# Loads of x in 2 KB instead of 8 KB descriptors, on a newly planned order of a fused attention and feed-forward kernel

## The chip, the cores and the metric

One core of one Trainium2 chip. The metric is the time of one execution in microseconds (us) on the device, lower is better. Before: 150.68 us as the median of 3 runs (150.09 to 151.19). The runs of this kernel scatter with the clock that TensorE is granted; a run is called fast when it is within 1.5% of the fastest of the same kernel, and ratios are taken over fast runs alone.

## The reference

```python
def _attn_ref(x, inducing):                 # x (4, 12480, 128), inducing (32, 128)
    def mab(q, kv):
        s = scale * (q @ kv.transpose(0, 2, 1))
        a = softmax(s)                      # cut: written out with max, exp, sum
        return a @ kv
    h = mab(I, x)                           # I: inducing for each of the 4 batches
    return mab(x, h)

def _moe_ref(x, w_in, w_out, alpha):        # 49920 tokens, d_ff 2048
    h = x @ w_in
    g = np.maximum(h, 0.0) + alpha * np.minimum(h, 0.0)
    return g @ w_out
```

The kernel reads x once (25.56 MB of float32), pools each batch into 32 rows, and then makes the output of each batch (25.56 MB in all) from the scores of x against those rows. A batch's outputs cannot begin before all of its x has been pooled.

## The kernel before

A batch is cut into seven chunks: six of 2048 rows (1 MB of x) and one of 192. For each chunk the first phase is: load with a cast to bf16 (POOL issues it), transpose ("flip") on DVE, scores on TensorE, exponential on ACT, sums on TensorE. The second phase makes scores again, exponentials, and the output, which DVE, or ACT with POOL, moves from PSUM into a buffer `ob` that SP stores.

The order of instructions is not written by hand. A small planner in the kernel plays the program through with its own costs, before anything is built, and writes each engine's instructions in the order that came out. On the chip each engine works in that order, whatever the real durations are.

```python
RINGS = dict(xn=12, xt=10, p=7, h=1, e1=3, e1t=3, g=3, ob=5)     # buffers
CAPS = dict(A=2, S=2, F=7, O=5)
class Plan:
    HOP = 0.12                              # us from one engine to another
    RATE = dict(L=424e3, S=400e3)           # bytes per us of loads, of stores
    SHARE = dict(L=0.8, S=0.2)              # when both run
    # ... cut: play() picks, again and again, the ready task of highest priority
TA, TS, TB, WL, LEAD = 4.0, 0.6, 4.2, 10, 0 # pace of the phases, sets priorities

def load(_):
    v["xn"] = ring("xn")                    # xn: [P, NK=16, C=128] bf16
    nc.gpsimd.dma_start(
        out=v["xn"][: c.p, : c.nk, :],
        in_=x[s.b, c.t0 : c.t0 + c.n, :].rearrange("(p j) c -> p j c", p=c.p),
    )

def flip(_):
    xT = ring("xt")
    nc.vector.transpose(out=xT[...], in_=v["xn"][: c.p, : c.nk, :].bitcast(f32))
```

A partition's 16 rows are contiguous in HBM and in SBUF, so a load is 128 descriptors of 8 KB read (4 KB written). A store's runs are 2 KB.

The softmax here doesn't subtract the row's maximum and nothing guards it: scores larger than these inputs give would overflow.

## Time and profile before

| | before |
|---|---|
| median of the first 3 runs | 150.68 us |
| profiled run (slow), span | 154.58, 152.3 us |
| x loads: issue on POOL, to landing (median) | 0.56 us, 11.3 us |
| DVE's idle time that x ended | 4.4 us |
| first and last output stored (issue) | 43.0, 143.8 us |

In the groups of instructions a row has the line, engine and operation, what it writes and reads, the count, the busy time in us and the mean of one in ns, and behind the last bar the idle time of the engine just before such an instruction, with what ended most of it. These rows are the flips and the issues of loads:

```profile
L472 DVE STREAM_TRANSPOSE xt<-xn 128x1024 f32<-128x1024 f32 (+1 forms) x28 | 29.8, 1075 | 4.4 <-DMA xn<-in_x_dram 4.4
L465 POOL DMA_DIRECT2D xn<-in_x_dram x28 | 15.6, 560 | 10.5 <-DMA xn<-in_x_dram 9.7
```

The prediction shows the rest: DMA full until the loads end, first with loads alone, then with loads and stores.

### The profile page before, as it was taken

The numbers are of one execution on the slowest core, as the hardware profiler recorded it, in microseconds if no ns is written. First come the engines' busy times: TensorE is split into PE (matmuls) and PEld (weight loads), VectorE is DVE, ScalarE is ACT, GpSimd is POOL, SyncE is SP. The second block draws the span as 40 slices with busy tenths as digits, with TensorE's granted clock in tenths as the row PEclk, the third lists the DMA queues.
The fourth block names the chain that finished last, engine by engine and source line by source line (L and its number), as shares of the span: only waits on it lengthen the run. The fifth ranks groups of instructions, "written<-read, shape, count | busy, mean of one in ns | idle before, by whom it ended". The sixth has DMA issues, their size and how long they took to land. (4 is left out here: it accounts for less than half of the span.)

```text
span 152.3 us, 5852 instructions
## 1 busy us (share of the span) xinstructions
PE 110.2 (72%) x2474; PEld 60.5 (40%) x2474; DVE 94.9 (62%) x251; ACT 77.6 (51%) x190; POOL 93.4 (61%) x119
## 2 busy tenths in 40 slices
PE   0019987999985876899969699798979994565100
PEld 0012434555543433545445364355653553443000
DVE  2069783489867964569876579928785846373300
ACT  3001422554875765353876647645964966646200
POOL 7821212920577979723697679614994897999700
PEclk9999999999999999689999999999996999655555
DMA  3999999999999999999999999998199888689991
GB/s 37 200 216 211 215 210 214 215 216 213 209 226 214 343 273 336 404 284 247 220 251 242 371 268 271 363 281 315 66 377 374 306 298 289 238 305 386 376 363 37
DMA packets 18063, 39.89 MB, mean 262 GB/s; under 512 B 1136, under 2 KB 2416, under 8 KB 18032
## 3 DMA queue, kind: packets, MB, share of 16 engines
q0 software_dynamic: 4192, 13.83, 47.0%
q1 hardware_dynamic: 13648, 25.57, 46.4%
q8 instruction: 21, 0.34, 0.8%
q10 hardware_dynamic: 192, 0.07, 0.2%
q14 instruction: 10, 0.08, 0.1%
HBM read 27.73 MB, written 25.56 MB: 350 GB/s over the span
## 5 line engine op out<-in xcount | busy, mean ns | idle before, releaser
L884 POOL TENSOR_TENSOR ob<-ob,rd 128x512 f32<-128x512 f32 (+1 forms) x78 | 72.2, 954 | 33.9 <-ACT ob L871 33.8
L871 ACT COPY ob<-p 128x512 f32<-128x512 f32 (+1 forms) x78 | 37.7, 549 | 15.2 <-PE p L854 9.6
L317 PE MATMUL p<-xt,ind_t 32*32 32x512 bf16 (+1 forms) x432 | 27.3, 366 | 12.6 <-DVE xt L472 11.6
L472 DVE STREAM_TRANSPOSE xt<-xn 128x1024 f32<-128x1024 f32 (+1 forms) x28 | 29.8, 1075 | 4.4 <-DMA xn<-in_x_dram 4.4
L317 PE MATMUL p<-xt,bh 32*32 32x512 bf16 (+1 forms) x432 | 29.0, 381 | 3.2 <-issue 2.9
L484 ACT ACTIVATE e<-p 128x512 bf16<-128x512 f32 (+1 forms) x28 | 15.1, 551 | 22.4 <-PE p L317 20.3
L465 POOL DMA_DIRECT2D xn<-in_x_dram x28 | 15.6, 560 | 10.5 <-DMA xn<-in_x_dram 9.7
L644 ACT ACTIVATE e<-p 128x512 bf16<-128x512 f32 (+1 forms) x28 | 15.2, 546 | 12.2 <-PE p L317 12.0
L869 DVE TENSOR_TENSOR ob<-p,rd 128x512 f32<-128x512 f32 (+1 forms) x30 | 19.1, 652 | 0.5 <-PE p L854 0.5
L849 PE MATMUL p<-zb,e 32*128 32x128 bf16 (+1 forms) x396 | 12.7, 231 | 8.9 <-ACT g L841 5.1
L317 PEld LDWEIGHTS <-ind_t 32*32 32x32 bf16 x432 | 9.3, 92 | 22.8 <-DVE ind_t L336 9.5
L834 DVE RECIPROCAL rd<-p 128x16 f32<-128x16 f32 (+1 forms) x28 | 6.7, 239 | 18.6 <-PE p L828 14.1
L317 PEld LDWEIGHTS <-bh 32*32 32x32 bf16 x432 | 10.4, 93 | 11.1 <-issue 4.2
L849 PEld LDWEIGHTS <-e 32*128 32x128 bf16 (+1 forms) x396 | 7.5, 98 | 14.8 <-issue 14.2
L492 DVE STREAM_TRANSPOSE e1t<-e 128x256 f32<-128x256 f32 (+1 forms) x28 | 10.5, 379 | 3.7 <-ACT e L484 3.7
L653 DVE SCALAR_TENSOR_TENSOR h<-e,h 128x256 int32<-128x256 int32 (+1 forms) x28 | 10.6, 379 | 2.9 <-PE h L512 1.4
L854 PE MATMUL p<-wb,g 32*128 32x512 bf16 (+1 forms) x108 | 11.6, 397 | 0.0
L502 PE MATMUL h<-xn,e1t 128*32 128x128 bf16 x392 | 10.4, 225 | 1.5 <-DVE h L653 0.9
L823 PE MATMUL p<-e,sp 128*128 128x128 bf16 (+1 forms) x100 | 10.9, 231 | 0.0
L841 ACT ACTIVATE g<-p 128x128 bf16<-128x128 f32 (+1 forms) x28 | 8.0, 287 | 4.3 <-DVE rd L834 4.3
L823 PEld LDWEIGHTS <-sp 128*128 128x128 bf16 (+1 forms) x100 | 6.3, 102 | 9.3 <-issue 8.9
L502 PEld LDWEIGHTS <-e1t 128*32 128x32 bf16 x392 | 6.4, 97 | 7.1 <-issue 2.5
(104 smaller groups left out, 108.2 us busy)
## 6 DMA issues: line engine op xcount, KB each, us to landing
out_dram<-ob SPq DMA_DIRECT2D x24, 1024.0 KB, 7.7
xn<-in_x_dram POOLq DMA_DIRECT2D x24, 512.0 KB, 11.3
w_in_b<-in_moe_w_in_dram POOLq DMA_DIRECT2D x1, 512.0 KB, 16.4
WO<-in_moe_w_out_dram POOLq DMA_DIRECT2D x1, 512.0 KB, 17.3
out_dram<-ob SPq DMA_DIRECT2D x4, 96.0 KB, 5.7
xn<-in_x_dram POOLq DMA_DIRECT2D x4, 48.0 KB, 11.2
ind<-in_inducing_dram ACTq DMA_DIRECT2D x4, 16.0 KB, 3.4
al<-in_moe_alpha_dram SPq DMA_DIRECT2D x1, 8.0 KB, 2.1
```

The lines of the kernel that those rows point to most:

```text
L317: nc.tensor.matmul(sc[rows, :], rows_t[rows, bb, :, e], xT[rows, : c.nk, bb, :, e], start=(n == 0), stop=(n == 3),)
L465: nc.gpsimd.dma_start(out=v["xn"][: c.p, : c.nk, :], in_=x[s.b, c.t0 : c.t0 + c.n, :].rearrange("(p j) c -> p j c", p=c.p),)
L472: nc.vector.transpose(out=xT[: c.p, : c.nk].rearrange("p k b j e -> p (k b j e)").bitcast(f32), in_=v["xn"][: c.p, : c.nk, :].bitcast(f32),)
L484: nc.scalar.activation(out=v["e1"][: c.p, : c.w].rearrange("p (K j e) -> p K j e", j=M, e=2), in_=v["sc"][: c.p, :].rearrange("p (K e j) - ...
L502: nc.tensor.matmul(h_all[q * M : (q + 1) * M, :], v["e1t"][: c.p, k // 2, :, k % 2], v["xn"][: c.p, k, :], start=(c.i == 0 and k < G), sto ...
L644: nc.scalar.activation(out=s.e2[: c.p, c.off : c.off + c.w].rearrange("p (r j k) -> p r j k", j=M, k=c.nkk), in_=w["sc"][: c.p, :].rearran ...
L823: nc.tensor.matmul(hh[:, : c.po], SP[r][: c.p, q].rearrange("p a q f -> p (a q f)"), e2(q), start=(q == 0), stop=(q == c.nq - 1),)
L849: nc.tensor.matmul(v["o"][a][: c.po, q * C : (q + 1) * C], e2(q, rows[a]), ZB[r][rows[a], :], start=(q == 0), stop=False,)
L854: nc.tensor.matmul(v["o"][a][: c.po, : c.nq * C], v["g"][rows[a], : c.po], WB[r][rows[a], : c.nq].rearrange("p q c -> p (q c)"), start=Fal ...
L869: nc.vector.tensor_tensor(out=ob, in0=o, in1=spread(rd), op=ALU.mult)
L871: nc.scalar.copy(out=ob, in_=o)
L884: nc.gpsimd.tensor_tensor(out=ob, in0=ob, in1=spread(s.rd[: c.po, c.i, : c.nq, a]), op=ALU.mult,)
```

## The change

The title names the descriptors, but two things change at once.

1. The tile of a load is padded, four runs of 512 elements and 2 spare ones each. A partition's 8 KB then cannot be one run in SBUF, and becomes four descriptors of 2 KB read and 1 KB written. The intent is that loads and stores, taken in turn packet by packet, share the DMA engines equally.
2. The order is planned anew: TensorE's results cost 0.2 us to another engine and a change of its tile mode 0.1, its groups are given other durations, filler matmuls stay in the running mode, rings and caps differ, and ten constants are set anew.

```diff
-RINGS = dict(xn=12, xt=10, p=7, h=1, e1=3, e1t=3, g=3, ob=5)
-CAPS = dict(A=2, S=2, F=7, O=5)
+RINGS = dict(xn=10, xt=14, p=7, h=1, e1=3, e1t=3, g=3, ob=5)
+CAPS = dict(A=2, S=3, F=7, O=5)
-LATE = 90.0
-AP = -0.2
-BIAS = 0.4
+LATE = 55.0
+AP = 0.0
+BIAS = 0.8
-    HOP = 0.12
+    HOP = 0.07
+    DRAIN = 0.2
+    SWITCH = 0.1
...
+                if eng == "PE":
+                    end += self.SWITCH if t["mode"] != self.mode else 0.0
+                    self.mode = t["mode"]
...
-        xn=([P, NK, C], bf16), ...
+        xn=([P, 4, NK // 4 * C + 2], bf16), ...
-    FB = 10.0
+    FB = 3.0
-    TA, TS, TB, WL, LEAD = 4.0, 0.6, 4.2, 10, 0
+    TA, TS, TB, WL, LEAD = 4.0, 1.2, 5.0, 6, 1
...
+        def rows_of(xn, c):
+            return xn[: c.p, : c.nkk, : c.nq * C]
-                out=v["xn"][: c.p, : c.nk, :],
-                in_=x[s.b, c.t0 : c.t0 + c.n, :].rearrange("(p j) c -> p j c", p=c.p),
+                out=rows_of(v["xn"], c),
+                in_=x[s.b, c.t0 : c.t0 + c.n, :].rearrange("(p k r) c -> p k (r c)", p=c.p, k=c.nkk),
...
-        XP = 10.0
+        XP = 40.0
... (cut: the planner's durations of the TensorE groups, each with its mode now)
```

SHARE stays at 0.8 and 0.2: the planner still believes that a load beside a store gets four fifths.

## The prediction

> **What bounds the kernel now.** I began with the page's row of DMA use by slice and the row of GB/s under it. A load counts there with the bf16 bytes that it writes, half of what it reads from HBM.
>
> ```profile
> PE   0019987999985876899969699798979994565100
> POOL 7821212920577979723697679614994897999700
> PEclk9999999999999999689999999999996999655555
> DMA  3999999999999999999999999998199888689991
> GB/s 37 200 216 211 215 210 214 215 216 213 209 226 214 343 273 336 404 284 247 220 251 242 371 268 271 363 281 315 66 377 374 306 298 289 238 305 386 376 363 37
> ```
>
> A slice is 3.8 us. From slice 2 to slice 28 the 16 DMA engines are full, to about 105 us. Until 43 us only loads run, at some 212 GB/s written, 424 read. Then loads and stores share. After the last load (landed at 103.5 us) only stores are left and the DMA row has holes: there the making of outputs is the bound. I then cut the span at those points with the view of busy time by stretch (PE, PEld, DVE, ACT, POOL, clock, DMA share, GB/s):
>
> ```profile
> 24.00:43.00 19.00, 17.45 (x368) 9.23 (x369) 14.51 (x35) 10.13 (x24) 8.84 (x9) 1.00 1.07 214
> 43.00:75.00 32.00, 26.32 (x653) 14.87 (x656) 21.92 (x57) 18.67 (x49) 21.54 (x27) 0.95 1.03 288
> 75.00:104.00 29.00, 24.82 (x618) 13.79 (x614) 20.77 (x53) 18.18 (x44) 20.70 (x25) 1.00 1.04 294
> 104.00:112.00 8.00, 6.53 (x188) 3.95 (x186) 6.26 (x21) 6.24 (x17) 6.06 (x7) 1.00 0.54 197
> 112.00:130.00 18.00, 15.59 (x315) 8.71 (x311) 11.98 (x38) 12.06 (x32) 14.30 (x17) 0.91 0.87 314
> 130.00:144.00 14.00, 6.80 (x114) 4.51 (x112) 6.07 (x14) 7.26 (x19) 12.91 (x14) 0.52 0.91 337
> ```
>
> Before 104 us the DMA share is 1.03 to 1.07. Behind it no engine sits at its limit: each waits for another in a fixed order. In the last 14 us POOL is busy 12.91 of 14. This profile fell in a slow state (154.58 us, against 150.68 as the median of the timed runs), and the granted clock of 0.52 at its end is part of that; I take some 4 us off the tail in a fast run.
>
> The third view is the DMA view of single stretches: loads alone (8 to 18 us), both (89 to 93), stores alone (112 to 119). Columns: packets, MB, share of 16 engines.
>
> ```profile
> q0 software_dynamic: 582, 2.12, 105.7%
> ```
> ```profile
> q0 software_dynamic: 170, 0.63, 77.9%
> q1 hardware_dynamic: 171, 0.35, 25.6%
> ```
> ```profile
> q1 hardware_dynamic: 1322, 2.61, 102.1%
> ```
>
> Queue 0 is the loads, queue 1 the stores. When both have work they take turns packet by packet, 170 to 171, and since a load packet reads 8 KB and a store packet carries 2 KB, loads get four fifths of the traffic (78% of the time against 26%).
>
> **What the Trainium skill says.** "DMA: Bandwidth & Descriptors", section "Queues, rings and completion order", says that each DMA engine goes round its queues at packet granularity; 170 against 171 agrees. The same page, "Why small descriptors are slow", gives a fixed overhead of about 3 cycles a packet, and the page's table a fabric of 32 bytes a cycle at 850 MHz on each engine. By that a 2 KB packet takes 67 cycles, 78.8 ns, and an 8 KB one 259 cycles, 304.7 ns: the trace has 309 (10 us x 16 / 517 full packets) for 8 KB, close, but 88 for the stores' 2 KB (7 us x 16 / 1274), more than the page's. "TensorEngine Tiling (Array Packing)", "Key Properties", says that changing the tiling mode drains TensorE. This trace does not isolate it; the planner in the new kernel now charges 0.1 us for it.
>
> **The change, part by part.**
>
> *Descriptors.* 24 full x loads have 128 packets of 8 KB, 8 per DMA engine and load, 192 in all: 192 x 309 ns = 59.3 us. They become 768 of 2 KB. At the page's 79 ns that is 60.5 us, at the stores' 88 ns 67.6. The stores write HBM and loads read it, so I choose 82, an estimate: 63.0 us, **+3.7 us of DMA time**. 14 full loads land before 46 us, where only loads run and DVE and TensorE follow them closely: 14 x 8 x 19 ns = 2.1 us on the path. The other 1.6 us fall where DMA is full too, so they move the last load as well.
>
> *Shares.* With equal packets loads and stores get half each. The total of bytes is the same, so where DMA is full this only changes the order: stores land sooner, loads later. At 103.5 us some 1.5 MB of stores were still under way; with equal shares perhaps half of that, so the last load is later by 0.75 MB / 380 = **+2 us**. Nobody waits in the trace for an output buffer, so faster stores free nothing.
>
> *Issue.* POOL takes 530 to 540 ns for a load of 128 descriptors and 522 to 530 for one of 96. From that slope 512 would cost about 0.12 us more (an estimate), 3 us over all loads, beside other work.
>
> *The new plan.* The order view shows the same sequence with small moves: 16 loads before the first output in both, the last load issued about one output earlier, one more output group after the last sums of the pooling. One output's transfer fewer ahead of the last load is 1.05 MB / 375 = **-2.8 us** there, and up to one chunk more in the tail, where a chunk takes 40 us / 14 = 2.9: zero in sum. Evictions by POOL fall from 78 to 70, by DVE they rise from 30 to 37, one is done by ACT in four scaled pieces. In the last two batches POOL loses 2 of 31 large ones, 2 x 1.05 = **-2 us** where it is the busiest engine.
>
> *Truer costs of TensorE in the planner* (drain 0.2 instead of 0.12 us to another engine, 0.1 for a mode switch, shorter sums). These cannot speed an instruction, only put fewer waiting instructions at the head of a queue. Waits of that kind between 43 and 104 us, from the view of waits: 10.9 us DVE reciprocal for TensorE, 9.1 us ACT exponentials for TensorE, 4.9 us ACT evictions for TensorE, 25 us over two engines. If a sixth to a third of one engine's 12 goes, in a stage where DMA is full, it earns only 0 to 2 us; in the tail as much again. I book **-3 us** together.
>
> Sum: +3.7 +2 (last load) +0 -2 -3 = +0.7 us. That these plan constants were tuned, in part to two digits, suggests more gain than I can count; I take off 2 for it, a judgement and no measurement. 150.7 - 1.3 gives about **149.4 us**.
>
> **Rivals.**
> 1. *Loads become the bound.* If a 2 KB load packet costs the stores' 88 ns, loads take 8.3 us more and the last one lands at 108 or later; nothing in the tail gives that back, so 153 to 156 us. For it: the measured 88. Against: reading and writing HBM need not cost the same.
> 2. *Sharing helps.* While both queues work the GB/s row dips (44 to 48 us, where the DMA view gives some 310 GB/s with loads counted by what they read), which could come from unlike packets. If equal packets lift the mixed stage from 380 to 400, 60 us become 57, and with the plan's gain the time is 145 to 147.
> 3. *Transfers hidden, tail alone decides.* DVE waits for x only 4.4 us in all, so later loads may be absorbed by the deeper ring of transposed tiles (14 instead of 10); then the time follows the POOL evictions alone: 147 to 149.
>
> **Range and chances.** The middle is 149.4, rivals 2 and 3 lie below and rival 1 above: 145 to 154 should hold it 8 times in 10. 2% is 147.7 and 153.7. Faster by over 2%: 0.30; within: 0.51; slower: 0.19.
>
> **What would show each step.** In loads alone, the GB/s row should fall from 212 to about 200 (82 ns); 188 means 88 ns and rival 1. In mixed stretches packets stay 1:1 but the two queues' shares should be alike. POOL's mean for an issue should be 0.65 to 0.7 us; over 1 us breaks that step. The last load should land at 104 to 107 us. POOL's busy share in the last 14 us should fall. The prediction is wrong if load packets overlap so well that the loads-only rate stays at 212, if a late load stops DVE for many microseconds in the mixed stage, or if the tail's order, which I judged by counts alone, moves the first output of the last batch by more than 3 us.

## The result, and the profile after

The changed kernel takes **157.05 us** (median of 4, 156.0 to 158.41) against 150.94 of the kernel before on the same chip, ratio **1.040** (95%: 1.030 to 1.051), slower. A ratio is the mean time of one kernel's fast runs over that of the other's fast runs of the same rounds, so it is not quite the ratio of the medians.

This profile is of a fast run, that of before of a slow one, so differences in the tail are not read from this pair. First the use by slices:

```profile
DMA  3999999999999999999989999995689988979991
GB/s 30 196 205 207 207 216 204 205 206 208 204 272 244 376 278 341 303 287 254 208 237 184 255 250 214 300 393 149 236 300 338 376 335 300 330 252 385 375 358 39
```

Loads alone bring 204 to 208 GB/s (one slice 216) where they brought 209 to 216. The busy row is as full as before, though what it moves behind slice 16 is less (184 to 255 in slices 19 to 25, 70 to 97 us). Part of that is the counting: loads are counted with half of what they read. Then the stretches (us; busy time of PE, PEld, DVE, ACT, POOL; clock, DMA share, GB/s):

```profile
24.00:43.00 19.00, 16.93 (x368) 8.56 (x369) 13.13 (x33) 9.18 (x21) 8.98 (x8) 1.00 1.24 205
43.00:75.00 32.00, 26.06 (x639) 14.35 (x638) 22.04 (x56) 18.32 (x47) 21.70 (x25) 0.95 1.13 292
75.00:104.00 29.00, 23.32 (x505) 12.30 (x502) 20.44 (x52) 14.06 (x34) 15.90 (x17) 0.82 1.09 252
130.00:144.00 14.00, 7.67 (x153) 5.49 (x151) 8.85 (x23) 8.29 (x21) 12.51 (x13) 0.70 0.91 330
```

The third row is where the time goes: from 75 to 104 us TensorE does 505 matmuls where it did 618, and ACT 34 instructions instead of 44. Work is missing in the middle, not slower at the end. The granted clock in this row is 0.82, against 1.00 before. The page has it low in slices 24 to 26 (0.7, 0.5, 0.5), just behind two slices in which TensorE worked half of the time, so I take it for a consequence of the waits; that is not shown, and it is a part of the loss either way. It is not all of it: the late-loads run below loses 2.9% with 0.94 in this stretch. The packets of loads alone (8 to 18 us), and of both together (69 to 70.5 us):

```profile
q0 software_dynamic: 2077, 2.06, 124.1%
```
```profile
q1 hardware_dynamic: 143, 0.29, 56.8%
q0 software_dynamic: 140, 0.14, 55.6%
```

2.06 MB instead of 2.12 in 10 us is 2.8% less. The two queues still send equal numbers of packets, 143 to 140, and their shares are now alike. (The records of small packets overlap: 2077 of them add up to 124% of the engines' time.) The groups of the flips and of the load issues:

```profile
L482 DVE STREAM_TRANSPOSE xt<-xn 128x1024 f32<-128x1024 f32 (+1 forms) x28 | 30.3, 1086 | 15.3 <-DMA xn<-in_x_dram 15.3
L475 POOL DMA_DIRECT2D xn<-in_x_dram x28 | 21.3, 761 | 9.7 <-DMA xn<-in_x_dram 5.0
```

DVE stood idle for 15.3 us until a load had landed, against 4.4; a load's issue costs POOL 0.76 us instead of 0.56. The timeline of DVE shows the longest of these stops (start, duration, what; idle time before it in brackets):

```profile
56.85 0.40 DVE L663 SCALAR_TENSOR_TENSOR h<-e,h 128x256 int32<-128x256 int32 x1
61.70 1.25 DVE L482 STREAM_TRANSPOSE xt<-xn 128x1024 f32<-128x1024 f32 x1 [4.45 <-DMA xn<-in_x_dram]
```

In the same place the kernel before had its flip behind a wait for TensorE, after the load had landed:

```profile
61.97 0.17 DVE L834 RECIPROCAL rd<-p 64x4 f32<-64x4 f32 x1 [2.65 <-PE p L828]
62.07 1.20 DVE L472 STREAM_TRANSPOSE xt<-xn 128x1024 f32<-128x1024 f32 x1
```

DVE works in its fixed order. While it stands before a flip, every reciprocal, eviction and transpose behind that flip stands too, and POOL, ACT and TensorE wait for those.

I then took the k-th load and the k-th flip of the trace together, for the 12 loads issued after 42 us (11 in one plan below). The **lead** is the time from the load's issue to the start of its flip:

| | lead, mean us | issue to landing, mean us | flips that started within 0.12 us of the landing | last load landed |
|---|---|---|---|---|
| before | 10.6 | 9.9 | 2 of 12 | 103.5 |
| changed | 11.3 | 10.5 | 8 of 12 | 107.8 |

Both orders leave a load hardly more time than it needs; in the changed kernel most flips start at the moment at which the load lets them. Its 8 KB twin, the first run below, has 9.3 us from issue to landing on the same order, so the descriptors alone delay a late load by some 1.2 us.

### The profile page after: what moved, and what is told of

Its sections match the earlier page's. It is cut to its first block, busy times and chain, and to the rows that moved or that the text cites.

```text
span 155.5 us, 5827 instructions
## 1 busy us (share of the span) xinstructions
PE 112.6 (72%) x2472; PEld 60.9 (39%) x2472; DVE 99.1 (64%) x263; ACT 75.5 (49%) x181; POOL 93.5 (60%) x111
## 4 chain that ended last, share of the span: by engine, by line
PE 33%; DMA 26%; DVE 11%; POOL 8%; ACT 8%; issue 7%; POOLq 0%; ACTq 0%; DVEq 0%
DMA xn<-in_x_dram 26%; PE p L324 18%; POOL ob L894 5%; PE p L859 4%; ACT ob L881 4%; PE p L864 3%; POOL xn L475 2%; PE p L833 2%; PE h L512 2%; DVE h L663 2%; DVE xt L482 2%; ACT g L851 2%; ACT e L654 1%; DVE ob L879 1%; ACT e L494 1%
## 5 line engine op out<-in xcount | busy, mean ns | idle before, releaser
L894 POOL TENSOR_TENSOR ob<-ob,rd 128x512 f32<-128x512 f32 (+1 forms) x70 | 66.7, 979 | 38.5 <-ACT ob L881 32.1
L482 DVE STREAM_TRANSPOSE xt<-xn 128x1024 f32<-128x1024 f32 (+1 forms) x28 | 30.3, 1086 | 15.3 <-DMA xn<-in_x_dram 15.3
L324 PE MATMUL p<-xt,ind_t 32*32 32x512 bf16 (+1 forms) x432 | 29.9, 396 | 13.1 <-DVE xt L482 10.1
L881 ACT COPY ob<-p 128x512 f32<-128x512 f32 (+1 forms) x70 | 34.7, 563 | 9.2 <-PE p L864 7.0
L324 PE MATMUL p<-xt,bh 32*32 32x512 bf16 (+1 forms) x432 | 28.4, 379 | 0.4 <-ACT e L494 0.2
L475 POOL DMA_DIRECT2D xn<-in_x_dram x28 | 21.3, 761 | 9.7 <-DMA xn<-in_x_dram 5.0
L879 DVE TENSOR_TENSOR ob<-p,rd 128x512 f32<-128x512 f32 (+1 forms) x37 | 21.5, 607 | 1.6 <-PE p L864 1.6
L324 PEld LDWEIGHTS <-ind_t 32*32 32x32 bf16 x432 | 10.5, 96 | 24.8 <-issue 11.2
L859 PE MATMUL p<-zb,e 32*128 32x128 bf16 (+1 forms) x396 | 11.9, 231 | 6.3 <-ACT g L851 5.8
L512 PE MATMUL h<-xn,e1t 128*32 128x128 bf16 x392 | 11.0, 229 | 5.4 <-DVE h L663 3.1
L324 PEld LDWEIGHTS <-bh 32*32 32x32 bf16 x432 | 9.6, 93 | 9.5 <-issue 2.8
L502 DVE STREAM_TRANSPOSE e1t<-e 128x256 f32<-128x256 f32 (+1 forms) x28 | 10.5, 384 | 4.4 <-ACT e L494 4.4
L859 PEld LDWEIGHTS <-e 32*128 32x128 bf16 (+1 forms) x396 | 7.4, 98 | 12.3 <-issue 11.3
L833 PE MATMUL p<-e,sp 128*128 128x128 bf16 (+1 forms) x100 | 11.3, 234 | 0.2
L512 PEld LDWEIGHTS <-e1t 128*32 128x32 bf16 x392 | 6.6, 99 | 11.3 <-issue 4.7
```

Source lines behind the costliest of these rows:

```text
L324: nc.tensor.matmul(sc[rows, :], rows_t[rows, bb, :, e], xT[rows, : c.nk, bb, :, e], start=(n == 0), stop=(n == 3),)
L475: nc.gpsimd.dma_start(out=rows_of(v["xn"], c), in_=x[s.b, c.t0 : c.t0 + c.n, :].rearrange("(p k r) c -> p k (r c)", p=c.p, k=c.nkk),)
L482: nc.vector.transpose(out=xT[: c.p, : c.nk].rearrange("p (k r) b j e -> p k (r b j e)", k=c.nkk).bitcast(f32), in_=rows_of(v["xn"], c).bit ...
L512: nc.tensor.matmul(h_all[q * M : (q + 1) * M, :], v["e1t"][: c.p, k // 2, :, k % 2], v["xn"][: c.p, k // c.nq, k % c.nq * C : (k % c.nq + ...
L833: nc.tensor.matmul(hh[:, : c.po], SP[r][: c.p, q].rearrange("p a q f -> p (a q f)"), e2(q), start=(q == 0), stop=(q == c.nq - 1),)
L859: nc.tensor.matmul(v["o"][a][: c.po, q * C : (q + 1) * C], e2(q, rows[a]), ZB[r][rows[a], :], start=(q == 0), stop=False,)
```

## The experiments

18 kernels ran. Medians are of all runs, ratios of fast runs against the kernel before on the same chip. Quotients of two ratios set side by side runs that were measured at different times, in part on different chips.

### Which half of the change costs: 8 KB on the new plan, 2 KB on the old

The first run undoes the padding and keeps the new order:

```diff
-        xn=([P, 4, NK // 4 * C + 2], bf16)
+        xn=([P, 4, NK // 4 * C], bf16)         # and the views accordingly
```

> The changed kernel with its x loads put back to 8 KB descriptors (no padding), its new plan kept; the order of instructions on each engine is the same. Theory S (equal shares make loads late in the mixed stage, and the in-order vector engine stops at the flips): about 150 to 152 us, waits of DVE for x back from 15.3 to under 7 us, packets still 1:1 but the loads' share four fifths. Theory P (the new plan itself is worse, whatever the descriptors): 155 to 157 us. Theory O (cost per packet and per issue): also 151 to 153, so it is told from S by the next runs.

Measured: 154.72 us, ratio 1.012 (1.008 to 1.016). DVE's wait for x was 10.5 us, not under 7 (the profile is of a slow run):

```profile
L483 DVE STREAM_TRANSPOSE xt<-xn 128x1024 f32<-128x1024 f32 (+1 forms) x28 | 30.0, 1079 | 10.5 <-DMA xn<-in_x_dram 10.5
```

So the new plan is itself slower by about 1.2%, some 1.8 us, and already sits close to its loads. The second run pads the tile in the kernel before and leaves its plan alone:

> The kernel before with 2 KB descriptors alone. Theory S: slower by 3 to 6 us, 154 to 157 us, with DVE waiting for x 10 us or more. Theory P: 151 to 152, no worse than a loads-only rate 3% lower makes it. Theory O: 152 to 153.

Measured: 157.44 us, ratio 1.028 (1.017 to 1.040); DVE waited 13.1 us for x, 7.3 of them after 43 us:

```profile
L475 DVE STREAM_TRANSPOSE xt<-xn 128x1024 f32<-128x1024 f32 (+1 forms) x28 | 30.4, 1088 | 13.1 <-DMA xn<-in_x_dram 13.1
```

The descriptors cost about 2.8% on the old plan, 4.2 us of 151. The changed kernel is 1.040 / 1.012 = 1.028 above its own plan with 8 KB. Two costs, about 1.2% and 2.8%, make up the 4%.

### When the descriptors cost: before the first store, or beside stores

In the changed kernel the 2 KB form was kept for two batches only, first for 0 and 1, whose loads come before or just as the stores begin, then for 2 and 3:

```diff
 def rows_of(xn, c):
+    if s.b >= 2:                                # the other run: s.b < 2
+        flat = xn[: c.p].rearrange("p k w -> p (k w)")[:, : c.nk * C]
+        return flat.rearrange("p (k w) -> p k w", k=c.nkk)   # 8 KB
     return xn[: c.p, : c.nkk, : c.nq * C]
```

> The changed kernel with 2 KB descriptors only for batches 0 and 1, whose loads land before the first store is issued; 8 KB for batches 2 and 3. Only the overhead of packets and issues in the loads-only stage is left: first store at 43.6 us as in the changed kernel. Theory S: within 1 us of the 8 KB version of the new plan. Theory O: half or more of the loss, 153 to 155.

> The changed kernel with 8 KB descriptors for batches 0 and 1 and 2 KB for batches 2 and 3, the loads that share the DMA engines with stores. Theory S: nearly all of the loss of the changed kernel, 155 to 157 us, with DVE waiting for x over 10 us behind 43 us. Theory O: half, about 153.

Measured: early loads alone 154.57 us, 0.998 (0.992 to 1.004; few of its 21 runs were fast, and its median is that of the 8 KB version); late loads alone 156.49 us, 1.029 (1.019 to 1.038), DVE waiting 13.0 us for x, all of it after 43 us:

```profile
L485 DVE STREAM_TRANSPOSE xt<-xn 128x1024 f32<-128x1024 f32 (+1 forms) x28 | 30.1, 1080 | 13.0 <-DMA xn<-in_x_dram 13.0
```

Against the 1.012 of the same plan with 8 KB, the late loads alone cost 1.7%. On the old plan the same, with late loads alone in 2 KB:

> The kernel before with 2 KB descriptors only in the loads of batches 2 and 3, which run beside stores. Equal shares as cause: most of what the same kernel loses with 2 KB everywhere (2.8%), so 1.5 to 2.8% slower, last load landing at 106 us or later. Packet overhead by itself: a third of it, under 1%.

Measured: 155.47 us, 1.017 (1.011 to 1.023). Its last load landed at 104.5 us and not at 106 or later (a slow run's profile), so that sign failed. The late loads alone make 1.7 of the 2.8% on both plans. The other 1.1% came on both plans only where the early loads were in 2 KB too (1.040 against 1.029, 1.028 against 1.017, with intervals that overlap); but on the new plan early loads alone in 2 KB were 1.4% faster than 8 KB (0.998 against 1.012). Whether the early ones cost anything is not settled.

### Is it POOL's longer issue?

```diff
             nc.gpsimd.dma_start(out=v["xn"][...], in_=...)      # 8 KB, the kernel before
+            if c.nk == NK:
+                nc.gpsimd.memset(idle[:], 0.0)                  # about 0.2 us
```

> The kernel before, 8 KB loads, with one small memset on POOL (about 0.2 us) right after the issue of each of the 24 full loads: the longer issue of a 2 KB load (0.74 against 0.54 us) without its packets. If POOL's issue time is a cause: slower by 2 us or more (24 x 0.2 = 4.8 us of POOL work). If equal shares are the cause: within 0.7 us of the kernel before.

Measured: 151.55 us, 0.992 (0.986 to 0.998). Making the issue longer (24 memsets of 0.23 us) costs nothing; that a run with more work came out faster I take for scatter. This profile is of a fast run with the order of the kernel before, so it is the better companion of the changed kernel's: its last load landed at 100.7 us, and the flips' row is

```profile
L476 DVE STREAM_TRANSPOSE xt<-xn 128x1024 f32<-128x1024 f32 (+1 forms) x28 | 30.3, 1087 | 5.1 <-DMA xn<-in_x_dram 5.1
```

So the old order waits about 5 us for x in a fast run as well.

### Changing the share from the other side

If the share of bytes decides, smaller packets of stores should help the loads. The stores of batches 0 and 1 were issued in two halves of 1 KB descriptors:

```diff
+        if plan.now and b < 2 and c.nq == 4:
+            for k in range(2):
+                w = slice(k * 2 * C, (k + 1) * 2 * C)
+                nc.sync.dma_start(out=dst[:, :, w], in_=src[:, :, w])
+            return
```

> The kernel before, 8 KB loads, with the stores of batches 0 and 1 (those that run beside loads) issued as two halves of 1 KB descriptors. Shares move the other way, 8 to 1 in bytes for the loads. If the share decides: the last load lands by 102 us, and the kernel is as fast as before or up to 1% faster. If small packets by themselves cost: 1% or more slower, as half of the mixed stage's bytes now have twice the packets.

> 2 KB loads on the old plan (2.8% slower by itself), and the stores of batches 0 and 1 in 1 KB descriptors: the loads' share is two thirds instead of half, and there are more packets than in any other version. If the share decides: better than 2 KB alone, 1.0 to 2.0% slower than the kernel before. If packets by themselves cost: 3.5% or more slower.

Measured: with 8 KB loads 152.92 us, 1.003 (0.999 to 1.007), DVE's wait for x 2.5 us; with 2 KB loads 156.07 us, 1.028 (1.017 to 1.038). The first is no gain. Its last load landed at 100.6 us, inside the expectation, but the run with memsets has it at 100.7 with ordinary stores, so this sign tells nothing; and DVE's wait for x after 43 us was only 1.6 us there, so little was left to win. The second is what 2 KB loads cost without it: more than the share theory allowed, less than the packet theory asked, so neither held. The share did move as meant (188 load packets to 186 store packets from 69 to 70.5 us), and the last load landed a little earlier (105.7 us against 107.0), and DVE waited less (9.5 us against 13.1), but the time did not follow. This pair is a miss for the simple theory that the share alone makes the time.

### Why is the new plan slower with 8 KB loads?

The plan's change was split: the new costs of TensorE with the old constants and rings, and the old costs with the new constants and rings.

> 8 KB loads, the planner's new costs of TensorE (drain, mode switch, shorter matrix groups, filler in the running mode), but the old rings and the old plan constants. The new plan with 8 KB lost 1.2% in fast runs. If the constants and rings lose it: within 0.5% of the kernel before, or faster. If the new cost model loses it: 1% or more slower.

> The opposite half: 8 KB loads, the old costs of TensorE, with the new rings (xn 10, xt 14), the third score buffer and the new plan constants. If these lose the 1.2%: 1% or more slower, with DVE waiting for x about 10 us as in the new plan with 8 KB. If the cost model loses it: within 0.5%.

Measured: 156.91 us, 1.028 (1.022 to 1.033), and 156.4 us, 1.025 (1.020 to 1.030). Each half is worse than both together (1.012). Neither half "has" the loss. With the new constants alone 8 of 12 late flips started with their load's landing, as in the changed kernel, though its loads were in 8 KB: an order can be this tight without small descriptors. My guess was that the constants had been chosen for their costs, and that either without the other is an order that nobody chose. To test that, one constant of the kernel before was moved by an amount that says nothing about the chip:

```diff
-    HOP = 0.12
+    HOP = 0.11          # one run
-    TA, TS, TB, WL, LEAD = 4.0, 0.6, 4.2, 10, 0
+    TA, TS, TB, WL, LEAD = 4.0, 0.6, 4.3, 10, 0    # another
```

> The kernel before with one constant of its planner moved by 0.01 us (HOP 0.12 to 0.11), which tells nothing about the chip and only gives another order. If the old order is a selected one and any other loses: 1 to 3% slower. If orders of like quality are common: within 0.7%.

> The kernel before with another constant moved a little (TB 4.2 to 4.3), again only another order. If the old order is a selected one: 1 to 3% slower. If orders of like quality are common: within 0.7%.

Measured: 156.73 us, 1.031 (1.022 to 1.040), and 155.01 us, 1.012 (1.001 to 1.022). A hundredth of a microsecond in one assumption is worth 3%. The two neighbouring orders lose 1 and 3%, as expected if the order before is a chosen one. The planner's own total, its estimate and no time of a chip, had said as much: 135.1 us before, 134.6 for the new plan, 140.6 and 138.5 for these two, 138.3 and 138.8 for the two halves. By that estimate there was 0.3% to be gained by planning anew, and the chip gave 1.2% the other way.

A search over the old planner's constants for a lower total found 134.8:

> 8 KB loads, the old planner, its constants searched a little further by the planner's own total (0.3 us lower of 135). If that total orders kernels to a few tenths: 0.2% faster. If small steps in it mean nothing on the chip: anything from 1% faster to 1.5% slower.

Measured: 153.06 us, 0.998 (0.992 to 1.004), the same. This planner is at its end, and a few tenths of its total mean nothing on the chip.

### Is it that the plan expects another share?

First a third order with 2 KB loads (HOP 0.11 and the padding):

> A third order (the old planner with HOP 0.11, 3.1% slower than the kernel before with 8 KB) with 2 KB loads. If the descriptors' cost belongs to the loads: 5 to 6.5% slower than the kernel before. If it only hurts an order tuned to the other share: 3 to 4%.

Measured: 159.35 us, 1.051 (1.044 to 1.057), against 1.031 with 8 KB: 2% more from 2 KB on a third order as well, DVE's wait for x 15.2 us against 7.6. All three orders had been planned for loads that get four fifths. Now the planner was told of equal shares, and its constants were searched again for that:

```diff
-    SHARE = dict(L=0.8, S=0.2)
+    SHARE = dict(L=0.5, S=0.5)
-LATE = 55.0    AP = 0.0    BIAS = 0.8    FB = 3.0
+LATE = 54.54   AP = 0.02   BIAS = 0.27   FB = 6.33
-    TA, TS, TB, WL, LEAD = 4.0, 1.2, 5.0, 6, 1
+    TA, TS, TB, WL, LEAD = 3.64, 1.45, 4.82, 6.1, 1.96
     # also SLACK 0.71, PW 15.72, OB 0.16, HOLD 15.19, XP 27.19
```

> 2 KB loads with the new TensorE costs, a planner told that loads and stores share equally (0.5 and 0.5), and its constants searched anew for that. If the wrong share in the plan is why 2 KB lose: within 1.5% of the kernel before, DVE waiting for x under 7 us. If 2 KB loads cost by arriving late whatever the plan expects: 2.5% or more slower.

> The same plan for equal shares with 8 KB loads, which arrive earlier than it expects. If the plan's assumption decides: no better than its 2 KB twin, within 0.7% of it. If 2 KB loads cost by themselves: 1.5 to 3% faster than the twin.

Measured: with 2 KB loads **151.97 us**, 1.0035 (1.000 to 1.007); its twin with 8 KB 151.95 us, 1.001 (0.997 to 1.004). On this order the descriptors cost 0.3%, where they cost 2.8, 2.8 and 2% on the others. The flips' rows of the two, 2 KB first:

```profile
L482 DVE STREAM_TRANSPOSE xt<-xn 128x1024 f32<-128x1024 f32 (+1 forms) x28 | 30.1, 1076 | 3.8 <-DMA xn<-in_x_dram 3.8
```
```profile
L483 DVE STREAM_TRANSPOSE xt<-xn 128x1024 f32<-128x1024 f32 (+1 forms) x28 | 29.9, 1071 | 0.0
```

The table of leads shows how (loads issued after 42 us):

| | lead | issue to landing | released by the landing | last load | ratio |
|---|---|---|---|---|---|
| changed, 2 KB | 11.3 | 10.5 | 8 of 12 | 107.8 | 1.040 |
| plan for equal shares, 2 KB | 19.3 | 15.0 | 0 of 11 | 103.9 | 1.0035 |
| plan for equal shares, 8 KB | 19.4 | 8.5 | 0 of 11 | 94.5 | 1.001 |

On this order a 2 KB load beside stores takes 15 us from issue to landing, and the order gives it 19. (The same loads took 10.5 us in the changed kernel; a load that is issued earlier may stand longer behind others in its queue, so lead and landing do not move apart freely. Between them lie 0.8 us on average in the changed kernel and 4.2 here, but 0.7 in the kernel before as well: the average alone does not tell which flips wait.) The twin's loads land after 8.5 us, are all in by 94.5 us, 9 us earlier, and it gains nothing: there no flip waited for a load (0.0 above), and the rest of the order sets the time. The 3.8 us of the 2 KB run all lie before 43 us; after that DVE waited 11.4 us in the changed kernel and none here. The stretch from 75 to 104 us (2 KB loads) is full again, with 620 matmuls where the changed kernel had 505:

```profile
75.00:104.00 29.00, 25.74 (x620) 13.88 (x612) 20.94 (x55) 19.63 (x48) 20.12 (x22) 1.00 1.13 298
```

Two things had been changed for it, the share and the constants. The last pair of runs altered SHARE alone:

> The changed kernel (2 KB loads) with one number altered: the planner's share of loads beside stores is 0.5, not 0.8; no constant searched. If the share alone gives the lead: issue to use 15 us or more on average behind 42 us, DVE waiting for x under 7 us, and within 0.7% of its 8 KB twin, though both may be 1 to 3% slower than the kernel before, as orders with unsearched constants were. If the constants gave it: lead 11 to 12 us, and 2% or more slower than the twin.

> The 8 KB twin of the run with the share alone altered. If the share alone gives the lead: the same time as the 2 KB one within 0.7%. If not: 2 to 3% faster than it.

Measured: 2 KB 1.013 (1.002 to 1.024), 8 KB 1.010 (1.003 to 1.016), the twins within 0.3% in fast runs. The lead grew from 11.3 to 14.8 us, so somewhat under half of the growth came from the share alone and the rest with the constants. This is not clean: 4 of the 6 runs with 2 KB were slow, at 159.1 to 160.6 us, so its median is 159.62 against 154.78. Landing took 13.3 us of a lead of 14.8, and 5 of 12 flips still started with the landing; DVE waited 6.4 us for x where the twin waited none, and the two fast runs hardly show it. I do not explain the slow runs.

The planner in each kernel.py, played through without a chip, says what it had reckoned with for loads issued after 42 us of its own time: landing after 5.0 us and a lead of 5.9 in the changed kernel, 15.8 and 16.8 in the plan for equal shares, 12.8 and 13.8 with the share alone. Landing measured 10.5, 15.0 and 13.3 us, but 9.3 us with 8 KB loads on the changed kernel's order too. So four fifths was too hopeful for 8 KB loads as well, and a share of 0.5 may help as a margin as much as by being right; no run separates the two.

No version was faster than the kernel before by 2%; the lowest ratio, 0.992, is that of the added memsets on its own order. Two other orders tie with it, the searched one and the one for equal shares.

## Why the prediction was wrong

**What bounds the kernel, packets in turn, equal shares: right.** 143 to 140 packets and 56.8% to 55.6% are what it said, and so is the order of the stretches. One reading was wrong: the clock of 0.52 at the end is no mark of the slow state, for the fast run with memsets on the same order has 0.50 there.

**Descriptors: the sum was about right, its make-up was not.** It booked 3.7 us for packets and 2 for shares, 5.7 in all; 2.8% or 4.2 us was measured, on both plans. But a 2 KB load packet takes 79.5 ns (10 us x 16 / 2012 packets, from 2.06 MB), near the 78.8 that I had estimated from the page's figures and not my chosen 82, so four are 318 ns and 192 x 9 ns = 1.7 us is all that packets cost by this estimate. The rest, some 2.5 us by subtraction, I put down to late loads on a waiting DVE; it is what the late loads alone cost (1.7%), though these contain packets of their own. I had written the mechanism down only as a thing that would make the prediction wrong ("a late load stops DVE for many microseconds in the mixed stage"), and that it did.

**The step that failed** is the new plan: 0 for the order, -2 for POOL, -3 for truer costs, and -2 as a judgement that tuned constants hide a gain, -7 us together. Measured with 8 KB loads: +1.2%, +1.8 us. That is 9 us of error, more than the miss of 7.7. 150.7 + 1.8 + 4.2 = 156.7 is close to the 157.05 measured. The counts were right (POOL 78 to 70 evictions), and in the last stretch POOL was busy 12.51 of 14 us instead of 12.91; but an order's time does not come out of counts: HOP 0.11 alone moved it by 3%. The first output of the last batch was issued at 132.5 us, against 130.0 in the profile of before and 128.2 in the fast run with memsets. Which of the four terms was furthest off the runs do not tell; the judgement had nothing measured behind it. Constants in two digits show that an order was chosen; the kernel before had been chosen as well.

**Rival 3 was wrong for this order, and right for another.** The deeper ring did not absorb late loads: the plan had not used it to issue earlier, its lead being 11.3 us against 10.6. With a lead of 19 us, from rings of the same sizes, the same loads are hidden. **Rival 1** came nearest (153 to 156, measured 157) for a wrong reason, the packet's cost of 88 ns. **Rival 2** fell: from 43 to 104 us the two queues together move 378 GB/s before and 365 in the changed kernel, with loads counted by what they read.

**Smaller terms.** POOL's issue is 0.76 us, not 0.65 to 0.7, and the run with memsets found no harm in a longer one. The last load landed at 107.8 us, against a predicted 104 to 107; a fast run of the old order has it at 100.7, so the delay is 7 us where I had reckoned with 0.5 to 3.5.

**Left open:** what makes an order 1% better than its neighbour beyond the loads' lead; whether early 2 KB loads cost anything; why the share alone leaves so many slow runs; how much of the middle stretch's loss is its lower clock.

## What to carry to other kernels

Here the size of the descriptors set how two queues share the DMA engines (77.9% and 25.6% of their time with 8 KB loads, 55.6% and 56.8% with 2 KB), so changing it changed when transfers landed; an order fixed in advance should be planned for that share, with more time between issue and use than a shared transfer needs. Measure that lead against the time to landing first: with 4 us to spare the descriptor size cost 0.3% here, and with 0.6 to 1.5 us 2 to 2.8% on three orders, where an engine that works in a fixed order handed its late loads on to the others. And compare a re-planned order with a plan of nearly the same constants before crediting the idea behind it.

## What the Trainium skill lacked or had wrong

- "DMA: Bandwidth & Descriptors", section "Why small descriptors are slow": its 3 cycles a packet held for loads (79.5 ns measured for 2 KB read, 78.8 estimated from its figures); stores of 2 KB took 88, which the page does not tell apart.
- The same page, "Queues, rings and completion order", speaks of packets of some 9 to 17 descriptors. The two queues here sent equal numbers of descriptors (170 to 171 with 8 KB against 2 KB, 143 to 140 with 2 KB against 2 KB); that fits turns of one descriptor, which the counts alone do not prove. It does not draw the consequence that the shares of two queues follow their descriptors' sizes (77.9% and 25.6% of the engines' time, then 55.6% and 56.8%).
- The same page, "Anatomy of one DMA — SWDGE (gpsimd) path", says of descriptor generation that many can be emitted before the cost shows. From 128 to 512 descriptors a load's issue on POOL grew from 0.56 to 0.76 us.
- No page that I read gives the cost of an in-order engine standing at a late load: 15.3 us of idle DVE in the changed kernel and 4.4 before, with a lead of 11 us; 3.8 us with a lead of 19, none of it after 43 us.
- "TensorEngine Tiling (Array Packing)", "Key Properties": the drain at a change of mode. No run here isolates it.
